# Deferring the layernorm scale of two tiles, loading on two queues and sending two biases later in a fused attention/MLP kernel

## The chip, the cores and the metric

The kernel runs on one core of one Trainium2 chip. The metric is the device time of one execution in microseconds (us), taken as the median of several runs. A core has five instruction streams that run side by side and wait for each other through semaphores: TensorE (PE, matmuls; PEld is its weight load), VectorE (DVE), ScalarE (ACT), GpSimd (POOL) and SyncE (SP). SP does no arithmetic here; it issues DMA transfers. ACT can issue DMA transfers too, between its activations. An issuing stream waits in order: what stands behind a waiting DMA on the same stream waits with it.

## What is computed

The input x has 2048 rows of 512 numbers, all in float32. It is normalised row by row, and two branches use the result:

```python
xn = _layernorm(x)                                # (x - mean) / sqrt(var + 1e-5)
q, k, v = split(xn @ wqkv)                        # 32 heads of 16
logits = q . k[pos - 2*w] * 16**-0.5              # w = 0..7, a dilated window
s = (softmax(logits) . v[pos - 2*w]) @ wo
h = relu(xn @ w1 + b1) ** 2                       # 512 -> 1792
g = silu(h @ w2 + b2)
return x + s * g
```

A row's layernorm is a subtraction of its mean and a multiplication by one number, rs = (var + 1e-5)^-0.5. A matmul is linear, so the multiplication may be done before the matmul or on its result.

## The kernel before

The rows of x are handled as 16 tiles of 128 rows, called t = 0 to 15, and in pairs; "pair 10" is tiles 10 and 11 (`pair` and `pair_of_seven` are called with a = 2, 4, ... 14; tiles 0 and 1 stand ahead of them, written out by hand). Stage one makes q, k and v of every tile, pair by pair. Stage two is the MLP with the output projection, in four chunks of four tiles. The attention itself (products, softmax and sums on DVE, a generator called `attention`) is woven between the PE work of both stages: `pump` lets as much of it be issued as a running estimate of PE's and DVE's time allows.

Matmul operands are split into a high and a low part (fp32r), and each product is three passes over these parts; `high` is an ACT copy that rounds, `low` a subtraction on DVE or POOL, `split` both.

How a tile of stage one is made: `load_x` brings 128 rows; `bn_stats` and `bn_aggr` on DVE give mean and variance (`mv`); DVE adds 1e-5, POOL raises to -0.5 (`rs`); DVE subtracts the mean and multiplies by rs (`xn`). For tiles 0 to 3, PE then transposes xn into PSUM (`pxT`, a matmul with the identity `ident`), and ACT and DVE write the high and low part of the transposed tile into `xT[0]` (tiles 0 to 3 in one buffer, used again at the start of stage two by `up(0, f)`). For tile 0 the transposed tile is first copied out as plain float32, `x0` (xT0f in the profile), and the first product of the program, k of tile 0, is made of it and of the raw weights `wqraw1_0` to `wqraw1_3` (four pieces of the k columns, 128 rows of wqkv each): 8 matmuls of the group pq<-wqraw,xT0f. The transposes of tile 1 stand ahead of the last piece. `evacuate` copies a product from PSUM to a staging tile `stg` on ACT, and `store_qkv` sends pairs of tiles to the DRAM scratch tensors `sq`, `sk`, `sv`, from which `load_u` loads the attention's operands on ACT's queue. PE starts with `WARM` transposes of the identity into an unused bank while it waits for the first tile.

Every operation of PE, DVE, ACT and POOL passes through `Ordered`, which keeps it in program order on its engine; a helper records them, so they all have line 91 in the profile. Transfers sent with `queue` keep program order on SP as well. Those sent with `dma` alone may be moved ahead by the scheduler: b1 and b2 are written in the program after pair 12 (a == NT - 4), and in the profile SP issues them at about 10 us. `plan` is a table of what is done beside which step of which pair: `at(a, step, f, ...)` puts a call behind the PE work of that step. `next_w` (pairs 12 and 14, then in stage two) splits one block of w1 and w2, the low parts on POOL, and asks for a later block.

Of the kernel before, what the change touches and what calls it, by code (L numbers as in the profile page):

```python
# [15 lines left out]
P = 128  # L16
S = 2048
D = 512
# [28 lines left out]
WARM = 18  # L47
# [12 lines left out]
def body(ctx: ExitStack, tc: tile.TileContext, x, wqkv, wo, w1, b1, w2, b2, out):  # L60
# [103 lines left out]
    def load_wq(s, kt, tag=None):  # L164
        rows = wqkv[kt * P:(kt + (2 if tag else 1)) * P, s * 512:(s + 1) * 512]
        if tag is None:
            raws[s, kt] = piece(f"wqraw{s}_{kt}")
            dma(raws[s, kt], rows)
            return
        if kt == 0:  # L170
            raws[s] = att.tile([P, KT, 512], F32, name=f"wqraw{s}", tag=tag)
        dma(raws[s][:, kt:kt + 2], rows.rearrange("(k p) n -> p k n", p=P))
        for i in (kt, kt + 1):
            raws[s, i] = raws[s][:, i]
# [7 lines left out]
    load_wq(1, 0)  # L182
    load_x(1)
    for kt in range(1, KT):
        load_wq(1, kt)
# [19 lines left out]

    b1t = const.tile([P, NF], F32, name="b1t")
    b2t = const.tile([P, D], F32, name="b2t")

    sq = dram.tile([GR, S, CH], F32, name="sq")
# [236 lines left out]

    def norm(t):
# [9 lines left out]
        if t < STATS:  # L457
            halves = [slice(0, D // 2), slice(D // 2, D)] if t == 0 else [slice(None)]
            for i in halves:
                V.tensor_scalar(dst[:, i], src[:, i], mv[t][:, 0:1], rs[t], op0=OP.subtract, op1=OP.mult)  # L460
        else:
            A.activation(dst, src, AF.Identity, bias=shifts.pop(t), scale=rs[t])
        if t < 2:
            load_x(t + 4)
# [115 lines left out]
    def evacuate(t, s, ps, new=True):  # L580
        if t % 2 == 0 and new:
            new_stg(t, s)
        A.activation(stgs[s][:, :, t % 2], ps.rearrange("p (g c) -> p g c", g=GR), AF.Copy)
        if t % 2:
            store_qkv(t, s)
# [52 lines left out]
    stats(0)  # L638
    high(*wq_parts(1, 0))
    norm(0)  # L640
# [5 lines left out]
    stats(1)  # L646
# [6 lines left out]
    norm(1)  # L653
# [113 lines left out]
    at(8, 1, lambda u: start("v", u), 0)  # L767
    plan.setdefault((10, 2), []).append((release, "k"))
# [111 lines left out]
    for a in range(2, NT, 2):  # L880
        if a >= TPC:
            for t in (a, a + 1):
                queue(sx[t // TPC][:, :, t % TPC], xts[t].bitcast(F32))
        (pair_of_seven if a in SEVEN else pair)(a)
        if a == NT - 4:
            dma(b1t, b1.rearrange("(f p) -> p f", p=P))
            dma(b2t, b2[None, :].to_broadcast([P, D]))
# [203 lines left out]
```

## Time and profile before

| | us |
|---|---|
| median of 3 runs | 485.36 (485.15 to 486.0) |
| the profiled execution | 485.13 |
| its span (first to last instruction) | 483.1 |

| engine | busy us | share of the span |
|---|---|---|
| DVE | 423.0 | 88% |
| ACT | 240.0 | 50% |
| POOL | 225.3 | 47% |

The profile is of one execution; 2.0 us of its time lie outside the span. Times in the rows below are counted from the span's start. In a row of the timeline, the first number is the start, the second the time taken (of several instructions together when an x2 or more stands behind), then the engine, the line, the operation and output<-input; in brackets stands how long the engine was idle before and what it then waited for. SPq and ACTq are the issues of DMA transfers by SP and ACT; their time is that of the issue, not of the transfer. PE records overlap, since a matmul's end is modelled: the start of the next one tells more than the sum.

### The profile page before, as it was taken

How to read it: one execution, taken by the hardware profiler on the slowest of the kernel's cores; microseconds unless marked ns; L12 is line 12 of the kernel's file. 1: busy time of each engine (PE TensorE's matmuls, PEld its weight loads, DVE VectorE, ACT ScalarE, POOL GpSimd, SP SyncE). 2: the span in 40 equal slices, each digit the busy share in tenths (PEclk: the TensorE clock that was granted, in tenths of full speed). 3: DMA queues.
4: the chain of work that ended last, by engine and by line, in shares of the span. 5: the costliest groups of instructions: out<-in, count | busy, mean ns of one | idle time of the engine just before them, and what ended most of it. 6: DMA issues, size and time to landing. Idle time of an engine off the chain costs nothing.

```text
span 483.1 us, 6128 instructions
## 1 busy us (share of the span) xinstructions
PE 477.4 (99%) x2190; PEld 396.6 (82%) x2190; DVE 423.0 (88%) x352; ACT 240.0 (50%) x441; POOL 225.3 (47%) x178
## 2 busy tenths in 40 slices
PE   8999999999999999999999999999999999999996
PEld 5888888888888888888888888888888888888885
DVE  5978999899499899999999999999999999889133
ACT  5548798856566565273513345342234543423240
POOL 1459853116986699436543322434433345253210
PEclk9999999999999999999999999999999999999999
DMA  7899999998779996571627548071707725220321
GB/s 283 243 251 258 277 243 302 263 306 269 209 198 228 255 224 151 178 166 43 170 72 185 115 164 190 26 189 43 197 16 196 224 48 145 43 86 27 87 105 71
DMA packets 71002, 81.47 MB, mean 169 GB/s; under 512 B 6204, under 2 KB 55612, under 8 KB 70972
## 3 DMA queue, kind: packets, MB, share of 16 engines
q1 hardware_dynamic: 65788, 54.87, 41.3%
q10 hardware_dynamic: 5184, 26.22, 21.8%
q8 instruction: 17, 0.28, 0.2%
q14 instruction: 13, 0.11, 0.1%
HBM read 50.60 MB, written 27.32 MB: 161 GB/s over the span
## 4 chain that ended last, share of the span: by engine, by line
PE 98%; DMA 1%; DVE 0%; POOL 0%; issue 0%; ACT 0%; POOLq 0%
PE ph L91 32%; PE pb L91 32%; PE pm L91 12%; PE pq L91 9%; PE pw L91 9%; PE pv L91 4%; DMA x<-in_A_x 1%; PE pxT L91 0%; DVE z L91 0%; DVE st L91 0%; POOL rs L91 0%; DVE xn L91 0%; ACT xT0f L91 0%; DVE mv L91 0%; DVE rs L91 0%
## 5 line engine op out<-in xcount | busy, mean ns | idle before, releaser
L91 PE MATMUL pb<-w,h 128*128 128x512 f32 x672 | 160.1, 389 | 0.0
L91 PEld LDWEIGHTS pb<-w,h 128*128 128x128 f32 x672 | 126.1, 188 | 26.2
L91 POOL TENSOR_TENSOR h<-hf,h 128x512 fp32r<-128x512 f32 x46 | 67.7, 1473 | 157.5 <-ACT hf L91 157.5
L91 PE MATMUL ph<-xU,w 128*128 128x512 f32 x504 | 120.2, 389 | 0.0
L91 ACT ACTIVATE ph<-ph,b1t 128x512 f32<-128x512 f32 x56 | 37.0, 661 | 153.9 <-PE ph L91 144.0
L91 PEld LDWEIGHTS ph<-xU,w 128*128 128x128 f32 x504 | 94.6, 188 | 19.6
L91 DVE TENSOR_TENSOR pr<-k,q 128x2048 f32<-128x2048 f32 x32 | 78.7, 2460 | 3.2 <-DMA q<-sq 2.5
L91 DVE TENSOR_TENSOR pv<-v,L 128x2048 f32<-128x2048 f32 x32 | 77.3, 2417 | 3.8 <-POOL L L91 3.1
L91 DVE TENSOR_REDUCE L<-pr 128x128 f32<-128x2048 f32 x32 | 73.0, 2281 | 0.7
L91 DVE TENSOR_REDUCE v<-pv 128x256 f32<-128x2048 f32 x32 | 72.9, 2279 | 0.7
L91 PE MATMUL pw<-wot,oT 128*128 128x512 f32 (+1 forms) x204 | 45.9, 376 | 0.0
L91 PEld LDWEIGHTS pw<-wot,oT 128*128 128x128 f32 x204 | 36.8, 188 | 7.1
L91 POOL TENSOR_TENSOR w<-w1r,w 128x512 fp32r<-128x512 f32 x14 | 31.6, 2259 | 23.4 <-ACT w L91 23.2
L91 PE MATMUL ph<-xT,w 128*128 128x512 f32 x168 | 40.0, 389 | 0.0
L91 PEld LDWEIGHTS ph<-xT,w 128*128 128x128 f32 x168 | 31.5, 188 | 6.6
L91 PE MATMUL pm<-wq,S 128*128 128x512 f32 x144 | 36.8, 392 | 0.0
L91 ACT ACTIVATE h<-ph 128x512 fp32r<-128x512 f32 x56 | 33.5, 599 | 1.8
L91 PE MATMUL pq<-wq,xT 128*128 128x512 f32 x132 | 30.9, 393 | 0.0
L91 PEld LDWEIGHTS pm<-wq,S 128*128 128x128 f32 x144 | 26.2, 188 | 5.3 <-DVE S L91 0.4
L91 PEld LDWEIGHTS pq<-wq,xT 128*128 128x128 f32 x132 | 24.5, 188 | 5.9 <-ACT xT L91 0.7
L91 ACT ACTIVATE hf<-ph 128x512 f32<-128x512 f32 x46 | 27.4, 595 | 1.9 <-POOL h L91 1.9
L91 PE MATMUL pm<-wq,xt 128*128 128x512 f32 x108 | 27.6, 392 | 0.0
(96 smaller groups left out, 531.0 us busy)
## 6 DMA issues: line engine op xcount, KB each, us to landing
k<-sk ACTq DMA_DIRECT2D x8, 960.0 KB, 7.1
v<-sv ACTq DMA_DIRECT2D x8, 960.0 KB, 7.4
sx<-xt SPq DMA_DIRECT2D x12, 512.0 KB, 5.8
xU<-sx ACTq DMA_DIRECT2D x12, 512.0 KB, 5.9
x<-in_A_x SPq DMA_DIRECT2D x16, 256.0 KB, 6.4
sk<-stg SPq DMA_DIRECT2D x8, 512.0 KB, 4.3
sq<-stg SPq DMA_DIRECT2D x8, 512.0 KB, 7.5
sv<-stg SPq DMA_DIRECT2D x8, 512.0 KB, 5.0
```

The source lines that it names most:

```text
L91: return tc.keep_in_program_order(f(*a, **k))
```

## The change

1. Tiles 0 and 1 are made by `centre` in place of `stats` and `norm`: the mean is subtracted and nothing is multiplied. `deviation` makes rs after that, in a column of a new tile `scales`, and sends the column to a DRAM scratch row `rows_dram` (128 elements of 4 bytes).
2. `evacuate` multiplies q, k and v of these two tiles by rs on the way out of PSUM (a scale operand of the ACT copy).
3. `up(0, f)` still needs the normalised tiles, transposed, where rs lies along the free axis. So SP loads both rows of rs back, broadcast to all partitions (`rows`). At pair 10 `rescale` adds high and low part of a tile's transposed x on POOL (`full`) and multiplies by the row, also on POOL; at pair 12 `rescaled` splits the result into `xT[0]` again, high on ACT and low on POOL.
4. The four raw pieces of the k columns go on two queues: 0 and 2 on ACT's, ahead of its table load, 1 and 3 on SP's, behind x of tiles 0 and 1.
5. WARM goes from 18 to 15.
6. b1 and b2 are sent with `queue`, at the end of pair 10 (a == NT - 6).

```diff
@@ -44,7 +44,7 @@
 SEVEN = range(4, 16, 2)
 VSEVEN = range(6, 14, 2)
 
-WARM = 18
+WARM = 15
 WARM2 = 3
 
 TURN = 4
@@ -161,11 +161,11 @@
 
     raws = {}
 
-    def load_wq(s, kt, tag=None):
+    def load_wq(s, kt, tag=None, send=dma):
         rows = wqkv[kt * P:(kt + (2 if tag else 1)) * P, s * 512:(s + 1) * 512]
         if tag is None:
             raws[s, kt] = piece(f"wqraw{s}_{kt}")
-            dma(raws[s, kt], rows)
+            send(raws[s, kt], rows)
             return
         if kt == 0:
             raws[s] = att.tile([P, KT, 512], F32, name=f"wqraw{s}", tag=tag)
@@ -179,10 +179,9 @@
 
 
     load_x(0)
-    load_wq(1, 0)
     load_x(1)
-    for kt in range(1, KT):
-        load_wq(1, kt)
+    for kt in range(KT):
+        load_wq(1, kt, send=queue if kt % 2 else A.dma_start)
     for kt in (0, 2):
         load_wq(0, kt, "pr")
     load_x(2)
@@ -203,9 +202,12 @@
         for w in range(W - 1):
             G.memset(mask[:GR, :(W - 1 - w) * DIL, w], -1e9)
 
+    scales = const.tile([P, 2], F32, name="scales")
+    rows = const.tile([P, 2 * P], F32, name="rows")
     b1t = const.tile([P, NF], F32, name="b1t")
     b2t = const.tile([P, D], F32, name="b2t")
 
+    rows_dram = dram.tile([2, P], F32, name="rows_dram")
     sq = dram.tile([GR, S, CH], F32, name="sq")
     sk = dram.tile([GR, HALO + S, CH], F32, name="sk")
     sv = dram.tile([GR, HALO + S, CH], F32, name="sv")
@@ -444,6 +446,38 @@
         V.bn_stats(st, xins[t])
         moments(t, st)
 
+    def centre(t):
+
+        st = px.tile([P, 6], F32, name=f"st{t}", tag="st", bufs=2)
+        mv[t] = px.tile([P, 2], F32, name=f"mv{t}", tag="mv", bufs=2)
+        xn[t] = dst = px.tile([P, 2, D], F32, name=f"xn{t}", tag="xb", bufs=2)[:, 0]
+        src = xins.pop(t)
+        V.bn_stats(st, src)
+        V.bn_aggr(mv[t], st)
+        halves = [slice(0, D // 2), slice(D // 2, D)] if t == 0 else [slice(None)]
+        for i in halves:
+            V.tensor_scalar(dst[:, i], src[:, i], mv[t][:, 0:1], None, op0=OP.subtract)
+        load_x(t + 4)
+
+    def deviation(t):
+        rs[t] = scales[:, t:t + 1]
+        V.tensor_scalar_add(rs[t], mv[t][:, 1:2], 1e-5)
+        G.tensor_tensor(rs[t], rs[t], mhalf, op=OP.pow)
+        dma(rows_dram[t:t + 1, :].rearrange("a p -> p a"), rs[t])
+
+    fulls = {}
+
+    def rescale(t):
+
+        if t == 0:
+            dma(rows, rows_dram.rearrange("a p -> (a p)")[None, :].to_broadcast([P, 2 * P]))
+        fulls[t] = full = px.tile([P, KT, P], F32, name=f"full{t}", tag="x", bufs=4)
+        G.tensor_add(full, xt[t][:, 0].bitcast(F32), xt[t][:, 1].bitcast(F32))
+        G.tensor_mul(full, full, rows[:, None, t * P:(t + 1) * P].to_broadcast([P, KT, P]))
+
+    def rescaled(t):
+        split(xt[t][:, 0], xt[t][:, 1], fulls[t], G)
+
     def norm(t):
 
         src = xins.pop(t)
@@ -455,13 +489,9 @@
             dst = xn[t // 2 * 2][:, :, t % 2].rearrange("p a (k c) -> p k a c", k=KT)
             src = src.rearrange("p (k a c) -> p k a c", a=4, k=KT)
         if t < STATS:
-            halves = [slice(0, D // 2), slice(D // 2, D)] if t == 0 else [slice(None)]
-            for i in halves:
-                V.tensor_scalar(dst[:, i], src[:, i], mv[t][:, 0:1], rs[t], op0=OP.subtract, op1=OP.mult)
+            V.tensor_scalar(dst, src, mv[t][:, 0:1], rs[t], op0=OP.subtract, op1=OP.mult)
         else:
             A.activation(dst, src, AF.Identity, bias=shifts.pop(t), scale=rs[t])
-        if t < 2:
-            load_x(t + 4)
 
     def place(t):
         if t < TPC:
@@ -580,7 +610,8 @@
     def evacuate(t, s, ps, new=True):
         if t % 2 == 0 and new:
             new_stg(t, s)
-        A.activation(stgs[s][:, :, t % 2], ps.rearrange("p (g c) -> p g c", g=GR), AF.Copy)
+        scale = dict(scale=rs[t]) if t < 2 else {}
+        A.activation(stgs[s][:, :, t % 2], ps.rearrange("p (g c) -> p g c", g=GR), AF.Copy, **scale)
         if t % 2:
             store_qkv(t, s)
 
@@ -635,22 +666,22 @@
         low(*wq_parts(s, kt + 1), V)
 
 
-    stats(0)
+    centre(0)
     high(*wq_parts(1, 0))
-    norm(0)
+    deviation(0)
     xT[0] = xTa.tile([P, KT, TPC, 2, P], FR, name="xT0", tag="xT")
     place(0)
     pT = [psT(f"pxT0_{kt}") for kt in (0, 2)]
     for kt in range(KT):
         PE.transpose(pT[kt // 2][:, kt * P:(kt + 1) * P], xn[0][:, kt * P:(kt + 1) * P], ident)
-    stats(1)
+    centre(1)
+    deviation(1)
     low(*wq_parts(1, 0), V)
 
     x0 = hpool.tile([P, D], F32, name="xT0f", tag="h", bufs=4)
     for kt in (0, 2):
         cols = slice(kt * P, (kt + 2) * P)
         A.activation(x0[:, cols], pT[kt // 2][:, cols], AF.Copy)
-    norm(1)
     for kt in range(1, KT):
         split(*wq_parts(1, kt), V)
     high(xt[0][:, 0], None, x0.rearrange("p (k n) -> p k n", k=KT))
@@ -765,6 +796,9 @@
     for i in range(2):
         at(4, i, load_w, i)
     at(8, 1, lambda u: start("v", u), 0)
+    for t in range(2):
+        at(10, 1 + 3 * t, rescale, t)
+        at(12, 3 + t, rescaled, t)
     plan.setdefault((10, 2), []).append((release, "k"))
     plan.setdefault((10, 4), []).append((release, "q"))
 
@@ -882,9 +916,9 @@
             for t in (a, a + 1):
                 queue(sx[t // TPC][:, :, t % TPC], xts[t].bitcast(F32))
         (pair_of_seven if a in SEVEN else pair)(a)
-        if a == NT - 4:
-            dma(b1t, b1.rearrange("(f p) -> p f", p=P))
-            dma(b2t, b2[None, :].to_broadcast([P, D]))
+        if a == NT - 6:
+            queue(b1t, b1.rearrange("(f p) -> p f", p=P))
+            queue(b2t, b2[None, :].to_broadcast([P, D]))
     pump()
     lowh(1)
     p1ctx.close()
```

The change moves instructions at three places. The first is DVE's first rows, from the first tile's statistics on (st, mv: statistics of a tile; rs or scales: the factor; wq: high and low parts of weights). Before:

```order
L91 BN_STATS st0_155<-x0_121 128x6
L91 BN_AGGR mv0_157<-st0_155 128x2
L91 TENSOR_SCALAR rs0_158<-mv0_157 128x1
L91 TENSOR_SCALAR xn0_163<-x0_121,mv0_157,rs0_158 128x256 x2
L91 BN_STATS st1_175<-x1_125 128x6
L91 BN_AGGR mv1_177<-st1_175 128x2
L91 TENSOR_SCALAR rs1_178<-mv1_177 128x1
L91 TENSOR_TENSOR wq2_113<-wqraw1_0_123,wq2_113 128x512
L91 TENSOR_SCALAR xn1_186<-x1_125,mv1_177,rs1_178 128x512
```

And now:

```order
L91 BN_STATS st0_155<-x0_118 128x6
L91 BN_AGGR mv0_156<-st0_155 128x2
L91 TENSOR_SCALAR xn0_157<-x0_118,mv0_156 128x256 x2
L91 TENSOR_SCALAR scales_143<-mv0_156 128x1
L91 BN_STATS st1_175<-x1_120 128x6
L91 BN_AGGR mv1_176<-st1_175 128x2
L91 TENSOR_SCALAR xn1_177<-x1_120,mv1_176 128x512
L91 TENSOR_SCALAR scales_143<-mv1_176 128x1
L91 TENSOR_TENSOR wq2_110<-wqraw1_0_122,wq2_110 128x512
```

The centred tile now follows its mean at once, and the factor is made behind it, for tile 1 ahead of the first split of weights.

The second is SP's queue from x of tile 4 to the first store of k (sk). Before:

```order
L104 DMA x4_166<-in_A_x 128x512
L104 DMA x5_188<-in_A_x 128x512
L886 DMA b1t_146<-in_B_b1 128x14x1
L887 DMA b2t_147<-in_B_b2 128x512
L104 DMA sk_149<-stg0_1_210 128x8x128
```

And now:

```order
L104 DMA x4_162<-in_A_x 128x512
L466 DMA rows_dram_147<-scales_143 128x1
L104 DMA x5_181<-in_A_x 128x512
L466 DMA rows_dram_147<-scales_143 128x1
L473 DMA rows_144<-rows_dram_147 128x256
L104 DMA sk_149<-stg0_1_210 128x8x128
```

The two bias loads are gone from here (they stand 48 rows further on, behind the last store of pair 10), and the two stores of rs and the load that reads them back have taken their place ahead of the store of k.

The third is POOL from the last statistics of pair 10 to the weights of pair 14 (w0, w1: blocks of w1 and w2; stg: sums for k and v). Before:

```order
L91 TENSOR_TENSOR shift15_1028<-mean15_1026,rs15_1027 128x1
L91 TENSOR_TENSOR stg10_1_1086<-stg10_1_1086,stg10_0_1088 128x8x64
L91 TENSOR_TENSOR stg10_2_1087<-stg10_2_1087 128x4x64
L91 TENSOR_TENSOR w0_1320<-w1r0_593,w0_1320 128x512
L91 TENSOR_TENSOR w0_1320<-w2r0_594,w0_1320 128x512
L91 TENSOR_TENSOR stg12_1_1234<-stg12_1_1234,stg12_0_1236 128x8x64
L91 TENSOR_TENSOR stg12_2_1235<-stg12_2_1235 128x4x64
L91 TENSOR_TENSOR w1_1411<-w1r1_631,w1_1411 128x512
```

And now:

```order
L91 TENSOR_TENSOR full0_1150<-xT0_168 128x512
L91 TENSOR_TENSOR full0_1150<-full0_1150,rows_144 128x512
L91 TENSOR_TENSOR stg10_1_1086<-stg10_1_1086,stg10_0_1088 128x8x64
L91 TENSOR_TENSOR stg10_2_1087<-stg10_2_1087 128x4x64
L91 TENSOR_TENSOR full1_1217<-xT0_168 128x512
L91 TENSOR_TENSOR full1_1217<-full1_1217,rows_144 128x512
L91 TENSOR_TENSOR w0_1329<-w1r0_593,w0_1329 128x512
L91 TENSOR_TENSOR w0_1329<-w2r0_594,w0_1329 128x512
L91 TENSOR_TENSOR stg12_1_1243<-stg12_1_1243,stg12_0_1245 128x8x64
L91 TENSOR_TENSOR stg12_2_1244<-stg12_2_1244 128x4x64
L91 TENSOR_TENSOR xT0_168<-full0_1150,xT0_168 128x4x128
L91 TENSOR_TENSOR xT0_168<-full1_1217,xT0_168 128x4x128
```

Six operations are added: two ahead of pair 10's sums, two behind them, and two between pair 12's sums and the weights of pair 14.

## The prediction

> **What bounds the kernel now.** I read the page first, then the busy times by stage, then the chain of waits.
>
> ```profile
> PE 477.4 (99%) x2190; PEld 396.6 (82%) x2190; DVE 423.0 (88%) x352; ACT 240.0 (50%) x441; POOL 225.3 (47%) x178
> PE 98%; DMA 1%; DVE 0%; POOL 0%; issue 0%; ACT 0%; POOLq 0%
> 12.00:24.00 12.00, 12.00 (x58) 9.75 (x57) 11.28 (x26) 7.04 (x14) 4.85 (x13) 1.00 0.89 244
> 450.00:483.10 33.10, 29.26 (x141) 24.54 (x139) 8.67 (x14) 9.38 (x15) 3.87 (x3) 1.00 0.24 83
> ```
>
> In the stage rows the first pair after the stretch is PE's busy time. PE sets the end: it is full from 12 us on and loses 3.8 us in the last stretch, which the change doesn't touch. No matmul of use is removed. So the change can gain only what it takes from the head, and lose only where it makes PE wait later. The head, from the chain of waits:
>
> ```profile
> 0.73 2.71 DMA x<-in_A_x
> 3.47 0.70 DVE st L91
> 4.19 0.19 DVE mv L91
> 4.41 0.17 DVE rs L91
> 4.72 0.57 POOL rs L91
> 5.31 0.42 DVE xn L91
> 5.78 0.46 PE pxT L91 x2
> 6.26 0.39 ACT xT0f L91
> 6.70 2.84 PE pq L91 x6
> 9.54 0.48 PE pxT L91 x4
> 10.02 6.55 PE pq L91 x26
> ```
>
> x of tile 0 lands, its statistics go through DVE and POOL, the tile is normalised, transposed, copied, and PE starts its first product at 6.70. From there PE works on end: everything behind moves with that start.
>
> **The head, step by step.** The factor rs leaves the chain: xn can start where rs started, at 4.41 in place of 5.31. That is **-0.90**.
>
> Against it stand three prices. The rows for them:
>
> ```profile
> 1.35 4.10 PE L91 MATMUL warm<-ident 128*128 128x128 f32 x18 [1.35 <-POOL mhalf L91]
> 4.29 0.63 ACT L91 ACTIVATE wq<-wqraw 128x512 fp32r<-128x512 f32 x1 [2.28 <-DMA wqraw<-in_A_wqkv]
> 6.53 0.69 DVE L91 BATCH_NORM_STATS2 st<-x 128x6 f32<-128x512 f32 x1 [0.48 <-DMA x<-in_A_x]
> 7.21 1.98 ACT L91 ACTIVATE wq<-wqraw 128x512 fp32r<-128x512 f32 x3 [0.25 <-DMA wqraw<-in_A_wqkv]
> 7.23 0.19 PEld L91 LDWEIGHTS pq<-wqraw,xT0f 128*128 128x128 f32 x1 [0.24 <-DMA wqraw<-in_A_wqkv]
> 9.39 0.63 PE L91 MATMUL pxT<-ident,xn 128*128 128x128 f32 x4
> 15.14 0.99 PEld L91 LDWEIGHTS pq<-wq,xT 128*128 128x128 f32 x5 [0.23 <-DVE wq L91]
> 3.50:7.00 3.50, 3.02 (x15) 2.25 (x14) 2.20 (x6) 1.33 (x3) 0.56 (x1) 1.00 0.79 259
> 7.00:14.50 7.50, 7.50 (x29) 4.57 (x28) 6.92 (x16) 6.40 (x12) 0.96 (x1) 1.00 1.04 391
> ```
>
> First, x of tile 0 now shares the DMA engines from its first byte with the first weight piece, which ACT issues at the same time; before, that piece was issued behind it. Lower end: x lands as now, 0. Upper end: x lands where that piece did, 4.29 against 3.47, or 0.82. An issue took 0.59 on ACT and 0.38 on SP in the rows on SP's queue below, so x keeps a lead of some 0.2; I take **+0.25**, nearer the lower end.
>
> Second, the second weight piece. The first product would then start at 6.70 - 0.90 + 0.25 = 6.05, and its second piece is wanted 0.53 later (6.70 to 7.23 now), at 6.58. In the kernel before PE and ACT waited for that piece until 7.2, as the fourth transfer of SP's queue. It is now the third, and the third landed at 6.53 (x of tile 1, for which DVE waited 0.48). That covers it: **0**. Upper end: it is the fifth of both queues together; a 256 KB transfer takes 0.67 us at 391 GB/s and 1.0 at 259, so it would land at 7.9 to 8.2, PE would start the second piece 0.7 to 1.0 later than before, and the whole gain would be gone. For the lower end speaks that the engines were busy 0.79 of the time and moved 259 GB/s from 3.5 to 7.0 us with loads waiting behind, but 391 after: with one queue they were not full.
>
> Here a rule of the Trainium skill speaks against the change: DMA: Bandwidth & Descriptors, section "Issuing engines are not separate DMA queues", has all issuing engines feed the same 16 DMA engines, so a second queue saves only the time to issue. By that rule the piece comes fifth and the sum is a loss of about 0.85; the row's 259 against 391 GB/s leaves it open, and it stands as a rival below.
>
> Third, PE's speed. The 18 warm transposes took some 0.22 each (4.10 us), the four at 9.39 some 0.12 to 0.16 each: PE was at half speed at first and doubled in between. Four transposes moved 0.65 earlier may still be slow: 0 to 0.2 on the path; I take **+0.1**. Three warm ones fewer free PE at about 4.8 (1.35 + 15 x 0.22 and the last one's drain), ahead of the centred tile (4.41 + 0.42 + 0.25 = 5.1), so they delay nothing; that PE speeds up later because of it is a rival.
>
> From 6.70 on the chain is PE's rows without a gap (6.70, 9.54, 10.02): tile 1's shorter chain gains nothing of its own. It gives DVE time back, and PE's 0.23 wait for DVE at 15.14 may go; I count 0, and 0.2 in the best case.
>
> **SP's queue.** The bias loads leave the head and three small transfers come, the last of which waits for the round trip of the second store. SP's next work is the first store of k.
>
> ```profile
> 11.27 4.25 SPq L887 DMA_DIRECT2D b2t<-in_B_b  x1
> 15.62 0.38 SPq L104 DMA_DIRECT2D sk<-stg  x1
> 20.39 0.59 ACTq L91 DMA_DIRECT2D k<-sk  x1
> 23.01 0.60 ACT L91 ACTIVATE stg<-pq 128x512 f32<-128x512 f32 x1 [2.12 <-PE pq L91]
> b2t<-in_B_b SPq DMA_DIRECT2D x1, 256.0 KB, 7.3
> sk<-stg SPq DMA_DIRECT2D x1, 512.0 KB, 4.5
> ```
>
> Before, b2's issue held SP to 15.52. If the second store of rs goes out as late as that issue began, 11.27, and lands 7.3 later as b2 did, the read goes at 18.6, k's store at 19.0, and it lands 4.5 later at 23.5 instead of 20.1. ACT, which waits there to issue the load of k, has 2.12 idle behind it, so its next copy is about 1 us late; PE has three more accumulator banks and doesn't notice. **0**; with that cover gone, 1 us. At pair 10 the biases hold SP for 5 us or so (b2's 4.25 again), and the next load it has to issue there, w1, waits for POOL until 114.05: 0.
>
> **Pairs 10 to 14.** POOL gets six more operations of 128x512, ACT two copies and six scaled evacuations.
>
> ```profile
> 97.08 1.29 POOL L91 TENSOR_TENSOR stg<-stg,stg 128x512 f32<-128x512 f32 x1 [9.38 <-ACT stg L91]
> 111.01 3.04 POOL L91 TENSOR_TENSOR w<-w1r,w 128x512 fp32r<-128x512 f32 x1 [11.92 <-ACT w L91]
> 116.97 1.19 POOL L91 TENSOR_TENSOR stg<-stg 128x256 f32<-128x256 f32 x1
> 119.79 2.29 DVE L91 TENSOR_TENSOR pr<-k,q 128x2048 f32<-128x2048 f32 x1
> 120.17 3.07 POOL L91 TENSOR_TENSOR w<-w1r,w 128x512 fp32r<-128x512 f32 x1 [2.01 <-ACT w L91]
> 132.93 0.60 ACT L91 ACTIVATE hf<-ph 128x512 f32<-128x512 f32 x1 [1.54 <-POOL h L91]
> 133.42 0.59 ACT L91 ACTIVATE stg<-pm 128x512 f32<-128x512 f32 x1
> 134.87 1.52 PE L91 MATMUL pm<-wq,xt 128*128 128x512 f32 x6
> 100.33 1.28 DVE L91 TENSOR_TENSOR S<-Sf,S 128x512 fp32r<-128x512 f32 x2
> 102.51 1.52 PE L91 MATMUL pm<-wq,S 128*128 128x512 f32 x6
> ```
>
> A POOL operation of this size takes 1.29, and 3.07 where a DVE multiplication of two tiles in SBUF runs: they exclude each other, and either may wait. The first two pairs of operations fall into POOL's idle 9.38 and 11.92. The second of these, at 99.1 to 101.7, meets DVE's S at 100.33, whose first half PE wants at 102.51 + 2 x 0.23 = 2.0 after it ended (1.28 / 2 behind 100.33): one POOL operation of 1.29 ahead of it is covered, two cost 0.6.
>
> The last two come between 118.16 and 120.17, in an idle 2.01, and want 2 x 1.29 = 2.58. The second one then runs into DVE's pr at 119.79, which starts at 120.74 and ends at 123.0; POOL's next weights end at 123.0 + 1.29 = 124.3, not 123.24: POOL is 1.05 late, with weights queued up behind. ACT waits for POOL's h at the end of that queue (1.54 at 132.93), then evacuates pm at 133.42 to 134.01, and PE wants that bank at 134.87: 0.86 of cover. So 0 to 0.2; I take **+0.1**.
>
> **The sum:** -0.90 + 0.25 + 0.1 + 0.1 = -0.45. The profiled execution took 485.13 (a span of 483.1 and 2.0 around it), which gives 484.68; the median of the runs, 485.36, lies 0.23 above it, so **484.9** for the median. Differences under 0.2%, or 0.97 us, can hardly be told from no change here.
>
> **The rivals.** (1) *The whole head is won*: x of tile 0 lands as before, the second queue fills the engines, POOL's delay stays covered, and the wait at 15.14 goes: -0.90 - 0.2, 484.3. For it: the half-empty engines until 7.0. Against it: two transfers start together. (2) *The second queue adds nothing*: the second piece lands fifth, +0.85 with no gain left, 486.2. For it: the transfers share one set of engines, as the traffic of one stage has one rate. (3) *POOL's last two operations*, slower: if all 2.58 or, with both behind DVE multiplications, 2 x 3.07 = 6.1 less the idle 2.0 = 4.1 go to the chain, PE waits 1.7 to 3.3 at its product at 134.87. Less the head's 0.55 that is 486.5 to 488.1. It decides from a delay of 2.4 on (0.86 of cover, 0.55 of gain, 0.97 to be seen). Against it: the two fall beside reductions for the most part. (4) *PE stays slow*: the warm stretch is now 15 x 0.22 = 3.3 us with a gap of 0.3 to 0.8 behind it. If the doubling comes one such stretch later, at about 10 us, PE does the 4 us from 6 to 10 at half speed, +2.0, 486.9. Against it: before, too, there was a gap of 0.3 ahead of the first transposes.
>
> TensorE: Matmul & The Clock Gate in the Trainium skill, part 1, states that PE runs at half clock until about 3.4 us of sustained activity, in a window that runs freely; 15 transposes are at that edge, and 18 were above it. The trace agrees that the rate doubles some 4 us after the first matmul; by the rule, a late doubling can strike some executions and not others.
>
> **The chances.** The forecast 0.47, its own range 484.4 to 485.6; rival 1 0.25; rival 2 0.10; rival 3 0.10; rival 4 0.08. Faster by over 0.2%: rival 1 and the forecast's edge, 0.27. Slower: rivals 3 and 4, 0.18. Within: 0.55. The range for 8 in 10 cuts off the edges of rival 1 and the upper ends of 3 and 4: 484.0 to 486.7.
>
> **What would show it.** Right: xn right behind mv, no POOL row in the chain; first product at about 6.15, k of tile 1 at 10.2; in pair 14 the same gapless PE. Wrong: statistics of tile 0 at 4.2 or later (first price), a PE load waiting for wqraw after the first two matmuls (rival 2), pxT rows and first matmuls at twice their time (rival 4), an idle PE between 102 and 139 (rival 3), or ACT's load of k so late that q's load, and with it the first products of attention, move back.

## The result and the profile after

| | before | after |
|---|---|---|
| median of 5 runs each, us | 485.67 (485.15 to 486.0) | 491.06 (490.31 to 491.92) |
| ratio, with 95% interval | | 1.011 (1.0096 to 1.0125) |
| the profiled execution, us | 485.13 | 491.06 |
| its span, us | 483.1 | 489.2 |

The change made the kernel 5.4 us slower; 484.9 was predicted. The span grew by 6.1 us. To see where, each matmul's start in the profile after is set against the start of the same matmul before. The difference, PE's delay below, grows in three places: to 1.95 by 10.7 us, to 4.6 between 42 and 48 us (pair 4; 0.3 of it is made good at 59 us), and from 4.4 to 6.2 between 158 and 192 us (second stage). Then it stays.

The rows of busy time by stage carry the same. Columns: the stretch, its length, busy time of PE, PEld, DVE, ACT and POOL, PEclk, the DMA engines' share and their GB/s. The kernel before:

```profile
0.00:12.00 12.00, 10.17 (x40) 6.93 (x41) 6.72 (x15) 6.70 (x12) 2.25 (x9) 1.00 0.79 282
...
36.00:48.00 12.00, 12.00 (x55) 9.93 (x54) 9.84 (x15) 9.79 (x22) 10.83 (x13) 1.00 0.96 254
...
150.00:200.00 50.00, 50.00 (x222) 41.39 (x222) 47.16 (x32) 29.35 (x52) 37.46 (x22) 1.00 0.83 197
```

The kernel after:

```profile
0.00:12.00 12.00, 9.61 (x30) 6.24 (x31) 5.29 (x13) 4.75 (x8) 2.23 (x9) 1.00 0.85 319
12.00:24.00 12.00, 12.00 (x55) 9.17 (x55) 10.86 (x23) 8.48 (x15) 4.07 (x12) 1.00 0.38 95
...
36.00:48.00 12.00, 10.41 (x45) 7.68 (x43) 8.17 (x17) 6.52 (x14) 9.32 (x9) 1.00 0.89 278
...
150.00:200.00 50.00, 49.68 (x215) 39.48 (x214) 44.09 (x31) 27.66 (x51) 41.35 (x24) 1.00 0.85 208
...
450.00:489.20 39.20, 35.44 (x168) 29.67 (x166) 13.07 (x19) 12.82 (x21) 5.16 (x4) 0.99 0.25 81
```

At the end PE is idle for 3.76 us, much as before (3.84). From 12 to 24 us the DMA engines moved 95 GB/s; before they moved 244. And PE, full from 36 to 48 us before, now lacks 1.6 us there. The lost time in the head is for the most part not an idle PE but a slow one. PEclk doesn't show it, since it is the mean over what the trace's clock record covers, and that begins at 10.48 here (5.64 before). The timeline of PE, after, shows the speed itself:

```profile
1.35 3.46 PE L91 MATMUL warm<-ident 128*128 128x128 f32 x15 [1.35 <-POOL mhalf L91]
5.81 1.12 PE L91 MATMUL pxT<-ident,xn 128*128 128x128 f32 x4 [0.99 <-DVE xn L91]
6.97 4.57 PE L91 MATMUL pq<-wqraw,xT0f 128*128 128x512 f32 x6
```

The four transposes took 1.12 instead of 0.76, and six matmuls 4.57 instead of 2.84: PE was at half speed until about 10.5, where before it doubled at 5.64. DVE's row of tile 0's statistics shows the late x, "st<-x" now at 4.45 instead of 3.47, and xn right behind mv:

```profile
4.45 0.69 DVE L91 BATCH_NORM_STATS2 st<-x 128x6 f32<-128x512 f32 x1 [4.45 <-DMA x<-in_A_x]
...
5.40 0.61 DVE L91 TENSOR_SCALAR xn<-x,mv 128x256 f32<-128x256 f32 x2
```

So rs left the chain as meant (0.9 gained), x landed 0.98 later, and the first product began at 6.97 instead of 6.70.

**Pair 4.** SP's issues in the timeline after:

```profile
9.73 0.33 SPq L466 DMA_DIRECT2D rows_dram<-scales  x1
20.40 0.33 SPq L473 DMA_DIRECT2D rows<-rows_dram  x1
20.82 0.39 SPq L104 DMA_DIRECT2D sk<-stg  x1
...
29.83 7.64 SPq L104 DMA_DIRECT2D x<-in_A_x  x4
```

The DMA view from 0 to 40 us, in 40 slices of 1 us (GB/s), and the time from issue to landing of the transfers that read `scales`, the two stores of rs (shortest, median, longest):

```profile
GB/s 0 14 248 322 404 402 410 406 408 406 406 410 406 388 95 0 0 0 0 0 0 7 54 193 325 339 281 244 93 146 309 184 239 157 157 219 360 273 323 410
```

```profile
DMA to landing us min/median/max: 10.6/11.6/12.5
```

And the timeline of the engines that wait, ACT, DVE and PE, with one piece of the chain of waits, the first load of x from its issue to its landing:

```profile
27.17 0.60 ACTq L91 DMA_DIRECT2D k<-sk  x1
27.82 1.27 ACT L91 ACTIVATE stg<-pq,scales 128x512 f32<-128x512 f32 x2 [4.81 <-PE pq L91]
...
29.83 10.64 DMA x<-in_A_x
...
40.49 0.69 DVE L91 BATCH_NORM_STATS2 st<-x 128x6 f32<-128x512 f32 x1 [2.40 <-DMA x<-in_A_x]
...
45.65 1.19 PE L91 MATMUL pm<-wq,xt 128*128 128x512 f32 x4 [1.18 <-DVE xt L91]
```

The second store of rs, 512 bytes as 128 elements of 4 bytes, was issued at 9.73 and took 10.6 us to land; in the trace its last packet ran at 14.6, so 5.7 of these passed behind it. SP stood until 20.40 to issue the read of the row, and everything behind it in SP's queue stood too: from 15 to 21 us no transfer ran at all. The store of k went at 20.82 instead of 15.62, the load of k at 27.17 instead of 20.39. Four loads of x stand behind. In the kernel before, the timeline of SP and DVE has them so:

```profile
28.58 1.90 SPq L104 DMA_DIRECT2D x<-in_A_x  x4
...
33.56 0.70 DVE L91 BATCH_NORM_STATS2 st<-x 128x6 f32<-128x512 f32 x1 [0.38 <-DMA x<-in_A_x]
...
36.68 0.69 DVE L91 BATCH_NORM_STATS2 st<-x 128x6 f32<-128x512 f32 x1 [2.02 <-DMA x<-in_A_x]
```

There the first two were issued at 28.58 and 28.98, and DVE had them at 33.56 and 36.68. Now the first was issued at 29.83, only 1.25 later, but it took 10.64 us to land instead of 4.96, and DVE had it at 40.49. What moved beside it is the load of k: before, that one had landed at 28.18, ahead of the first x; now it was under way from 27.17 to 36.17. It also held up the other three: by the trace's semaphores SP issued the second at 36.18, when the load of k had landed, since it waits on the semaphore that this load sets. DVE had the second x at 41.51. Behind the two stood the transposed tiles of pair 4 (the first at 44.92 instead of 40.03), for which PE then waited.

The other profiles bear this out. In the six with both stores and the read in the head, the first x took 9.8 to 11.1 us with the load of k still moving; with only the stores there (a_read_late below) it took 9.3; in the eight others the load of k had landed 0.4 to 0.8 before that x was issued, and it took 4.1 to 5.5.

**Second stage.** Pieces of the chain of waits after, in order of time, and the waits from 155 to 194 us:

```profile
147.50 3.36 POOL w L91
150.87 8.54 DMA w2r<-in_B_w
...
159.43 0.52 ACTq L91
...
162.67 3.01 PE ph L91 x12
```

```profile
DVE h L91 <- ACT ph L91: 4.3, 1, 4.3
...
PEld ph L91 <- DVE h L91: 2.5, 6, 0.5
```

POOL's split of weights ends late, SP issues the next w2r behind it at 150.87, and that transfer takes 8.54. ACT's next instruction is the issue of the load of q, which waits until it has landed (159.43), and DVE stands 4.3 for ACT. What this delay then costs is seen in DVE's timeline:

```profile
173.03 0.68 DVE L91 TENSOR_TENSOR h<-ph,h 128x512 fp32r<-128x512 f32 x1
173.63 2.27 DVE L91 TENSOR_REDUCE L<-pr 128x128 f32<-128x2048 f32 x1
175.94 2.98 DVE L91 TENSOR_TENSOR pr<-k,q 128x2048 f32<-128x2048 f32 x1
178.84 0.68 DVE L91 TENSOR_TENSOR h<-ph,h 128x512 fp32r<-128x512 f32 x1
```

One round of DVE takes 5.81 (173.03 to 178.84), one of PE 5.44 (two groups of 12 matmuls, 2.72 each). Before, DVE came into this stretch with enough lead; now it comes late, and each round takes 0.2 to 0.4 from PE: 1.77 between 155 and 195 us.

### The profile page after: what moved, and what is told of

Read it like the earlier page. It is cut to its first block, busy times and chain, and to the rows that moved or that the text cites. A ratio compares the mean times of both kernels' runs of the same rounds, so it can differ in the third digit from the quotient of the medians.

```text
span 489.2 us, 6136 instructions
## 1 busy us (share of the span) xinstructions
PE 481.1 (98%) x2187; PEld 396.3 (81%) x2187; DVE 423.8 (87%) x352; ACT 241.1 (49%) x443; POOL 247.3 (51%) x184
## 4 chain that ended last, share of the span: by engine, by line
PE 78%; DMA 7%; DVE 5%; POOL 5%; issue 3%; ACT 1%; SPq 0%; ACTq 0%; DVEq 0%; POOLq 0%
PE pb L91 27%; PE ph L91 26%; PE pm L91 10%; PE pw L91 9%; PE pv L91 4%; DMA x<-in_A_x 3%; POOL w L91 3%; DMA w2r<-in_B_w 2%; PE pq L91 2%; DMA sq<-stg 1%; DVE L L91 1%; DVE h L91 1%; DVE st L91 1%; DMA w1r<-in_B_w 1%; POOL xT L91 1%
## 5 line engine op out<-in xcount | busy, mean ns | idle before, releaser
L91 POOL TENSOR_TENSOR h<-hf,h 128x512 fp32r<-128x512 f32 x46 | 76.7, 1667 | 145.4 <-ACT hf L91 142.2
```

The costliest lines, as they stand in the source:

```text
L91: return tc.keep_in_program_order(f(*a, **k))
```

## The experiments

The theory: three independent losses, (1) PE's doubling comes late because fewer warm transposes and the late x leave a gap, (2) SP's wait for the round trip of rs, (3) POOL's rescaling, or the biases, in the second stage. The rivals are named with each run. The kernel before ran beside them, with medians of 485.27 to 485.91 over 13 to 22 runs. "Delay" is PE's delay against the profile before, just ahead of pair 4 (41 us), behind it (70 us), at 155 us and at 195 us; "doubling" is the time from which PE stays at full speed in the head, by the trace's clock record.

| kernel | median (runs), us | ratio (95%) | doubling | delay at 41 | 70 | 155 | 195 |
|---|---|---|---|---|---|---|---|
| after | 491.06 (5) | 1.011 (1.0096 to 1.0125) | 10.48 | 2.00 | 4.31 | 4.41 | 6.18 |
| b_warm15 | 486.87 (10) | 1.0016 (0.9999 to 1.0033) | 10.60 | 1.90 | 1.68 | 1.68 | 1.91 |
| a_warm18 | 490.4 (4) | 1.0096 (1.0076 to 1.0117) | 4.16 | -0.15 | 3.09 | 3.16 | 4.53 |
| a_rows_late | 491.67 (4) | 1.0112 (1.0082 to 1.0141) | 5.23 | -0.11 | -0.39 | 6.74 | 6.74 |
| a_read_late | 488.67 (4) | 1.0056 (1.0035 to 1.0077) | 9.67 | 1.43 | 2.17 | 3.63 | 4.29 |
| a_bias_early | 491.1 (4) | 1.0102 (1.0064 to 1.0139) | 4.41 | 0.12 | 3.85 | 3.98 | 6.25 |
| a_no_pool | 488.88 (8) | 1.0057 (1.0037 to 1.0076) | 4.37 | 0.12 | 4.10 | 4.10 | 4.10 |
| a_one_queue | 490.46 (5) | 1.0096 (1.0065 to 1.0128) | 6.47 | -0.52 | 3.51 | 3.61 | 4.63 |
| b_two_queues | 487.92 (10) | 1.0036 (1.0009 to 1.0062) | 11.72 | 2.45 | 2.53 | 2.53 | 4.40 |
| a_no_trip | 486.33 (10) | 0.9998 (0.9981 to 1.0015) | 9.65 | 1.48 | 1.47 | 1.47 | 1.47 |
| f1 | 486.26 (12) | 1.0009 (0.9995 to 1.0024) | 6.52 | -0.09 | 0.70 | 0.69 | 1.11 |
| b_warm20 | 486.67 (12) | 1.0015 (0.9997 to 1.0033) | 5.16 | -0.10 | -0.10 | -0.10 | 1.50 |
| a_q_first | 488.6 (4) | 1.006 (1.0041 to 1.0079) | 10.47 | 1.95 | 3.49 | 3.58 | 5.24 |
| b_q_first | 485.91 (12) | 1.0012 (0.9999 to 1.0026) | 5.75 | -0.05 | -0.14 | -0.14 | -0.07 |

In b_two_queues PE was fast from 4.90 to 8.31 and slow again until 11.72. Where the runs fall into two groups, the ratio can differ by up to 0.16% from the quotient of the medians; its interval is what counts.

### The warm-up (b_warm15, a_warm18)

```diff
-WARM = 18
+WARM = 15
```

on the kernel before, and the reverse on the changed one.

> The kernel before with WARM 15 in place of 18 and nothing else. Theory (clock): in the changed kernel's profile PE ran at half speed to 10.5 us because 15 warm transposes leave too long a gap ahead of tile 0's. Here the gap is as long (4.6 to 5.8), so PE's first products should again stand 0.85 apart and not 0.43, and the time should rise by 1.0 to 2.0 us, to 486.7 to 487.7. Rival (chance): when PE doubles its rate is set by a phase that has nothing to do with the number of warm transposes; then 485.7, as before.

> The changed kernel with WARM 18 again. Theory (clock): the first products run at full speed, k of tile 1 starts some 1.7 us earlier than 12.67, and the time falls from 491.1 to about 489.4. Rival (the late first tile): the gap that x's late landing leaves is what counts, and three more transposes don't close it: 491.1.

The profile of the kernel before with 15 transposes shows PE's slow head alone, +1.9, with x landing as before:

```profile
6.93 4.64 PE L91 MATMUL pq<-wqraw,xT0f 128*128 128x512 f32 x6
```

Over its ten runs it is a matter of chance: three at 484.9 to 485.5, the rest from 486.0 to 487.9, and the interval of the ratio reaches below 1, so the runs alone don't show a rise. With 18 the changed kernel had its doubling at 4.16 and no delay in the head, and still took 490.4: the delay behind pair 4 was 3.1. (The profiled run, 489.41, is the fastest of its four.) So the head's loss and pair 4's don't simply add. A PE that comes 2 us earlier waits longer there for the transfers.

### The round trip (a_rows_late, a_read_late)

The stores and the read of rs moved to pair 8, each sent by a small function in SP's order (a_rows_late), or the read alone (a_read_late, without the lines on the stores):

```diff
-        dma(rows_dram[t:t + 1, :].rearrange("a p -> p a"), rs[t])
...
-        if t == 0:
-            dma(rows, rows_dram.rearrange("a p -> (a p)")[None, :].to_broadcast([P, 2 * P]))
...
+    at(8, 4, send_rows, 0)
+    at(8, 4, send_rows, 1)
+    at(8, 5, read_rows, 0)
```

> The changed kernel with both stores of rs and the load that reads them back moved to pair 8 in SP's queue. Theory (round trip): they hold up the first store of k, with it ACT, the loads of x and of q, and make PE wait 2.4 us at pair 4; here that wait is gone, the store of k is issued near 17 and not 20.8, and the time is 488.7, unless the round trip now holds SP in pair 8. Rival (scaled evacuations and the lost 2 us of the head make pair 4 late): the wait at pair 4 stays, 490.5 to 491.

> The changed kernel with the two stores of rs where they are, and only the load that reads them back moved to pair 8. It parts two forms of the round-trip theory. If SP's wait for the stores is what costs, the store of k is issued near 17 and the time is 488.7, as with both moved. If the stores themselves clog the DMA engines (in the profile x of tile 5 and both stores land only at 20 with hardly any traffic from 14 to 20), the store of k is issued early but lands no earlier than 24, and the time stays at 490 to 491.

With both late, the wait at pair 4 is gone (delay -0.11 to -0.39), and the loss is at 98 to 112 us instead (one of the four runs took 488.98, the others 491.6 to 492.0). Its waits there:

```profile
POOL full L91 <- DMA rows<-rows_dram: 14.1, 1, 14.1
ACT stg L91 <- POOL stg L91: 6.6, 1, 6.6
...
PE pv L91 <- ACT stg L91: 3.4, 2, 3.1
```

POOL stood 14.1 us for the row, ACT behind POOL, PE behind ACT; and after that gap PE ran at half speed from 107.6 to 114.4, PEclk 0.50 in the busy time by stage:

```profile
100.00:107.60 7.60, 5.46 (x30) 4.55 (x28) 7.57 (x8) 1.02 (x3) 4.72 (x3) 1.00 0.95 251
107.60:114.40 6.80, 5.80 (x20) 5.13 (x21) 2.58 (x5) 3.69 (x9) 3.27 (x3) 0.50 1.14 331
```

With only the read late, SP doesn't stand (the store of k goes at 15.91), and pair 4 costs 0.74 instead of 2.3: two thirds of it was SP's wait. The 0.74 that stays goes with the stores of 4-byte elements: the load of k was issued at 22.39 and landed at 32.58, again beside the first x. The median agrees with the 488.7 expected, but in part by chance: PE lost another 1.46 between 70 and 155 us, 1.1 of it at 118 to 121, after POOL had stood 7.9 us for the row at 91 to 99. The way from there to PE isn't shown.

### The second stage (a_bias_early, a_no_pool)

```diff
-        if a == NT - 6:
-            queue(b1t, b1.rearrange("(f p) -> p f", p=P))
-            queue(b2t, b2[None, :].to_broadcast([P, D]))
+        if a == NT - 4:
+            dma(b1t, b1.rearrange("(f p) -> p f", p=P))
+            dma(b2t, b2[None, :].to_broadcast([P, D]))
```

in a_bias_early, and in a_no_pool:

```diff
     def rescale(t):
...
+        return
...
     def rescaled(t):
-        split(xt[t][:, 0], xt[t][:, 1], fulls[t], G)
+        pass
```

> The changed kernel with b1 and b2 sent at pair 12, by the queue that takes turns, as before; all else as changed. The changed kernel showed a third loss of 1.75 us between 158 and 191 us, in steps of 0.25 to 0.37 at which the products ph wait for DVE's h. Theory A (the biases, sent two pairs earlier in SP's queue, hold back the load of w2r, which landed 8.54 us after its issue): the steps go, the offset of PE against the kernel before is the same at 195 us as at 155, and the time falls by 1.5 to 2 us. Rival B (POOL's rescaling of tiles 0 and 1 makes POOL late for the splits of the weights): the steps stay, and the time is within 0.5 us of the changed kernel's 491.06.

> The changed kernel without POOL's sums, products and splits of the two tiles' transposed x (the row of rs is stored and read back as changed; the transposed x of tiles 0 and 1 stays centred but unscaled for the second stage, which this kernel so leaves out). Theory B (POOL): the steps of 158 to 191 us go, and the time falls by 1.5 to 2 us to 489.0 to 489.6. Rival A (the biases at pair 10): the steps stay, and the time is within 0.5 us of 491.06. The wait at pair 4 stays in both cases, since the round trip through memory is kept.

The biases' place is not it: 491.1, and the second stage lost 2.3. Without POOL's work it lost nothing, and the median fell by 2.2. (a_no_pool leaves out ACT's two copies for the splits as well; that POOL is the one is read from the waits.) The way there begins in SP's issues behind the store of v. The timeline after:

```profile
141.73 0.53 SPq L104 DMA_DIRECT2D sv<-stg  x1
144.57 0.37 SPq L406 DMA_DIRECT2D w1r<-in_B_w  x1
```

And without POOL's work:

```profile
140.71 0.53 SPq L104 DMA_DIRECT2D sv<-stg  x1
141.69 0.47 SPq L406 DMA_DIRECT2D w1r<-in_B_w  x1
```

The next weights are asked for 2.84 behind the store of v instead of 0.98: SP waits there for POOL to free their buffer. Of the seven profiled kernels with POOL's rescaling six lost 0.7 to 2.3 us between 155 and 195 us (a_rows_late didn't).

The trace's semaphores show what this lateness meets. In all thirteen profiles in which, at 145 to 152 us, the load of k is issued ahead of that of q, ACT issued the load of q 0.02 to 0.03 us after one load of w2r had landed, on whose semaphore it waits. They fall into three groups (times in us):

| profiles | that w2r was issued | and took | q issued behind k by | lost between 155 and 195 |
|---|---|---|---|---|
| before, b_warm15, a_rows_late, a_no_pool, a_no_trip, f1 | 1.16 to 1.22 before k | 3.29 to 3.62 | 2.15 to 2.42 | 0 to 0.42 |
| b_warm20, b_two_queues | 1.22 before k | 5.43, 6.10 | 4.23, 4.91 | 1.60, 1.87 |
| a_read_late, a_one_queue, a_warm18, after, a_bias_early | 1.09 to 1.16 behind k | 7.29, 7.77, 8.52, 8.54, 9.04 | 8.42 to 10.15 | 0.66, 1.02, 1.37, 1.77, 2.27 |

With POOL late, this w2r comes behind the load of k (960 KB) instead of ahead of it and takes 4 to 6 us longer, and ACT stands at the issue of q for that time. In the last group the loss rises with it. a_rows_late has the rescaling, but its w2r came ahead of k, and it lost nothing there.

Pair 4 in a_no_pool, whose head lost nothing, by the timeline of PE and then the busy time:

```profile
44.83 1.66 PE L91 MATMUL pm<-wq,xt 128*128 128x512 f32 x4 [2.25 <-DVE xt L91]
```

```profile
45.30:48.70 3.40, 3.40 (x10) 2.15 (x9) 2.36 (x5) 3.07 (x8) 3.23 (x5) 0.50 0.89 178
```

PE came on time, waited 2.25, and soon after ran at half speed for 3.4 us. So an early PE lost as much at pair 4 as the late one lost in head and pair 4 together.

### The two queues (a_one_queue, b_two_queues)

```diff
+    load_wq(1, 0, send=queue)
     load_x(1)
-    for kt in range(KT):
-        load_wq(1, kt, send=queue if kt % 2 else A.dma_start)
+    for kt in range(1, KT):
+        load_wq(1, kt, send=queue)
```

in a_one_queue; b_two_queues does the reverse to the kernel before.

> The changed kernel with the first loads in the order of the kernel before and on SP's queue alone. Theory C (x of tile 0 shares the engines with the first piece that ACT sends at the same time): x of tile 0 lands at 3.4 to 3.6 instead of 4.42, and the first product starts 0.7 to 1.0 earlier, at 6.0 to 6.3; the time falls by 0.7 to 1.0 if the clock doubles as late as in the changed kernel, by up to 2.5 if it doubles early. Rival (x of tile 0 lands late for another reason, such as its place in the queue): the landing stays above 4.2. The wait at pair 4 stays.

> The kernel before with only the first loads changed to two queues. Theory C (shared engines): x of tile 0 lands 0.8 to 1.1 later, at 4.2 to 4.5, and since x leads the chain to the first product here too, the first product starts 0.8 to 1.1 later, at 7.5 to 7.8 instead of 6.70; the time is 486.1 to 486.7 with an early doubling of the clock. Rival (the loads in sum come sooner, and the chain from x is not the longest): the first product is within 0.2 of 6.70 and the time within 0.3 of 485.5.

The changed kernel with one queue, DVE and PE:

```profile
3.40 0.69 DVE L91 BATCH_NORM_STATS2 st<-x 128x6 f32<-128x512 f32 x1 [3.40 <-DMA x<-in_A_x]
...
5.92 3.10 PE L91 MATMUL pq<-wqraw,xT0f 128*128 128x512 f32 x6
```

The kernel before with two queues:

```profile
4.37 0.69 DVE L91 BATCH_NORM_STATS2 st<-x 128x6 f32<-128x512 f32 x1 [4.37 <-DMA x<-in_A_x]
...
6.68 0.77 PE L91 MATMUL pxT<-ident,xn 128*128 128x128 f32 x4 [1.44 <-DVE xn L91]
```

x of tile 0 lands 0.9 to 1.05 later with two queues, in either kernel: it is the second queue that makes it late. Over all profiles DVE had it at 4.13 to 4.52 with two queues (nine) and at 3.38 to 3.56 with one (six). With one queue the change does bring its product forward, to 5.92, and PE is 0.52 ahead at 41 us. Pair 4 takes it: the delay behind is 3.5, and the median falls by 0.6, less than the 0.7 to 2.5 expected. In b_two_queues the first product came at 7.59, as expected; its 487.92 lies above the 486.1 to 486.7 given for an early doubling, which its profile doesn't have. It also lost 1.87 in the second stage, with no rescaling in it; DVE there waited 4.6 for q, against 2.5 before. Of the eight profiled kernels without the rescaling this and b_warm20 (below) lost over 0.5 us there. So POOL is not the only way into this loss.

### Without the trip, and a version from the findings (a_no_trip, f1)

a_no_trip takes away both stores, the read and the rescaling. f1 is the kernel before with these lines:

```diff
-WARM = 18
+WARM = 15
-    stats(0)
+    centre()
...
-    norm(0)
...
+    PE.transpose(pT[1][:, 0:P], rs[0].to_broadcast([P, P]), ident)
+    A.activation(rows, pT[1][:, 0:P], AF.Copy)
+    G.tensor_mul(x0s.rearrange("p (k n) -> p k n", k=KT), x0.rearrange("p (k n) -> p k n", k=KT),
+                 rows[:, None, :].to_broadcast([P, KT, P]))
```

`centre` treats tile 0 alone, its k is scaled where it leaves PSUM, and x0s is split in place of x0.

> The changed kernel without the two stores of rs, the read of the row and POOL's rescaling: tiles 0 and 1 stay unscaled in the second stage, which this kernel so leaves out. What is left of the change is the head, the scaled evacuations and the place of the biases. If the losses at pair 4 and in the second stage come from the round trip and from POOL's rescaling alone, PE's offset against the kernel before stays below 0.3 us from 12 us to the end, apart from what the clock does in the head: a span of 482.9 to 483.6 where the clock doubles by 6.5 us, 484.7 to 485.4 where it doubles after 9.5. If the scaled evacuations or the biases have a share in the losses, a step of 0.5 us or more is left at 42 to 48 us or at 158 to 191 us.

> A version built from the findings: the kernel before with first loads on one queue as before, tile 0 alone centred first, its k scaled where it leaves PSUM, 15 warm-up transposes (so that PE goes from them to tile 0's without a gap); the row of rs is made by one transpose of rs in the head, and POOL scales the transposed x of tile 0 there, before it is split, so that there is no trip through memory and no later rescaling. Expected: first transposes at 4.8 instead of 5.78, first product at 6.0; k of tile 1 at 10.0 to 10.4 instead of 10.71 where the clock doubles by 6.5 us; no wait at pair 4 or in the second stage; 484.8 to 485.2, that is 0.3 to 0.6 below the kernel before. The rival is that the trip over POOL makes the split of tile 0 late for its q at 12.7 us, and PE gives the gain back there: 485.4 to 486.5.

Without the trip and the rescaling nothing is left of the losses but the head's doubling: the delay is 1.48 at 41 us and 1.47 at 195. Four of its ten runs lie at 484.86 to 485.28, where the faster runs of the kernel before lie too. So losses 2 and 3 of the changed kernel belong to trip and rescaling, and what is left of the change, with its late x, gains nothing that can be told (0.9981 to 1.0015).

f1 had its first product at 5.90 and was no faster. Its lead, 0.80 there, was 0.44 at the last matmul of tile 0's k (PE doubled at 6.52 instead of 5.64, and the transpose of rs stood between), and gone at the next (10.73 against 10.71), for which PE waited 0.30 for ACT, whose copy stood behind POOL's product. It then fell 0.8 behind at 44 and 59 us, where PE waited for S:

```profile
10.73 5.51 PE L91 MATMUL pq<-wq,xT 128*128 128x512 f32 x23 [0.30 <-ACT xT L91]
...
59.50 1.19 PE L91 MATMUL pm<-wq,S 128*128 128x512 f32 x4 [0.25 <-DVE S L91]
```

### What else spreads the runs (b_warm20, a_q_first, b_q_first)

b_warm20 is the kernel before with

```diff
-WARM = 18
+WARM = 20
```

and the other two are the changed kernel and the kernel before with

```diff
-                yield from load(u + 1, "kq")
+                yield from load(u + 1, "qk" if u == 1 else "kq")
```

> The kernel before with 20 warm-up transposes, which at 0.213 us each fill PE to 5.87 us, past tile 0's xn at 5.78: no gap is left. If the clock doubles at the end of a stretch of some 3.41 us, at a phase that differs by execution, in which PE was nearly without a gap (doublings seen: 4.2 to 6.5, or 9.7 to 10.6 where a gap of 0.7 to 1.0 lay in the stretch before), it now doubles by 7.7 us at the latest: the slower group of runs at 486.25 to 487.5, about a quarter of the runs of the kernel before, goes, and all runs lie within 484.8 and 486.2, the median at 485.0 to 485.6. If the spread has another cause, the slower group stays at its share of a quarter.

> The changed kernel with one pair of issues on ACT swapped: the load of q of the third unit (in the profiles at 148 to 160 us) ahead of the load of k, which stood just before it. In the kernels whose second stage lost time, the load of q was issued 4.2 to 10.2 us after that of k, against 2.2 to 2.4 in the others; theory D: the load of k starts while the store of q is still in SP's queue and takes the engines from it, the load of q waits for that store, ACT and DVE stand, and DVE's rounds of 5.8 us then hold PE, whose rounds take 5.44. With q first the store meets no load of k: q is issued within 1 us of where PE's own delay puts it (by 153), the steps between 158 and 191 us go, PE's offset at 195 us is within 0.3 of that at 150, and the time is 489.0 to 489.6. Rival E (the store of q is late because POOL's rescaling holds SP's queue, whatever the load of k does): q is issued 3 us late or more, now with k behind it, and the steps stay or grow: 490.8 to 493.

> The kernel before with the same swap. Theory D: it loses nothing where the store of q landed in time anyway, and the runs in which the second stage lost 1.5 us (as in the profiled runs with two queues and with 20 warm-up transposes) go: the median falls by 0 to 0.4, and the share of runs above 486.2 from a third to the share of late doublings of the clock, a fifth or less. Rival: the load of k, now 2.4 us later, lands after DVE wants it, and the time rises by 0.5 to 2 us.

b_warm20 missed: no gap was left worth the name (0.21) and the doubling came at 5.16, but its slower runs stayed. Its profile has the second stage's loss, 1.6, with DVE's wait as in b_two_queues:

```profile
DVE pr L91 <- DMA q<-sq: 4.7, 1, 4.7
PEld ph L91 <- DVE h L91: 2.2, 5, 0.5
```

So two things can differ by execution without the change, the doubling and this; the profile of the kernel before itself shows neither. a_q_first was to show that the load of k delays the store of q. q was issued at 148.87, in time, as the theory had it, yet the delay grew by 1.66 between 155 and 195 us, since ACT now waited 8.3 for w2r and DVE 4.3 for ACT: the theory that the order of these two loads makes the loss falls. The same w2r was issued behind both loads, at 149.98, and took 10.4. The median of a_q_first, 2.5 below the changed kernel's, rests on four runs in two groups (487.5 to 487.6, 489.6 to 490.4) and isn't explained. b_q_first changed nothing that can be told. By the table above, the transfer that decides whether DVE comes late to the second stage is that load of w2r; what stays open is why it took 5.4 and 6.1 us in the two profiles without rescaling, ahead of the load of k as in those that took 3.3 to 3.6. No version that beats the kernel before was found.

## Why the prediction was wrong

- **The head's gain, -0.90:** right. xn stands right behind mv, and no POOL row is in the chain.
- **The first price, +0.25 for x of tile 0:** too small; it measured 0.98, above the upper end of 0.82. The working gave x a lead of 0.2 from the times of issue. With two queues DVE had x 0.66 to 1.05 later than the 3.47 of before in each profile, with one queue on time, so most or all of the gain went here.
- **The second piece, 0:** right. PE waited for no wqraw, and the engines moved 319 GB/s in the first 12 us instead of 282. Rival 2 falls. The rule set beside it (the Trainium skill, DMA: Bandwidth & Descriptors, "Issuing engines are not separate DMA queues") was taken to mean that the piece comes fifth and late, which these rows don't show.
- **PE's speed, +0.1:** wrong in this execution; rival 4, with a chance of 0.08, came true, and its +2.0 was +1.7. Its condition was half seen: the doubling comes at a different time in each execution, and a gap behind the warm transposes goes with the late one: of nine profiles with a gap of 0.67 to 1.22 five doubled at 9.65 or later (not the two longest), of five with 0.41 or less none did. The late x widened the gap to 0.99, and the working never joined these two terms. The Trainium skill, TensorE: Matmul & The Clock Gate, part 1, has the freely running window of about 3.4 us; the half-speed stretch of 3.4 us in a_no_pool and the doublings between 4.2 and 11.7 agree with it.
- **SP's queue, "0; with that cover gone, 1 us":** the step that failed. It had the round trip nearly right, the read at 18.6 (20.40 measured) and the store of k at 19.0 (20.82). It then followed one transfer, the store and load of k, to ACT's idle time, and found cover. It stopped at the issue of the load of k (27.17 instead of 20.39) and didn't follow it to its landing, nor the queue behind: that load was now under way until 36.17, beside the first load of x, which landed at 40.47 instead of 33.54, and ahead of the other three, which SP could issue only when it had landed. PE has no cover for those. In this execution that was 2.3 us, and 3.2 to 4.0 where PE came on time.
- **Pairs 10 to 14, +0.1:** right for where it looked; PE lost 0.1 from 70 to 155 us. Rival 3 had POOL's work coming out at 134.87, in the products of stage one. It came out 25 us later, through a chain that wasn't in the working: POOL late, its buffers late, SP's load of w2r behind the load of k instead of ahead of it, ACT held at the issue of q until it landed, DVE late, and DVE's rounds of 5.81 against PE's 5.44. It measured 1.77.
- **The sum** put three losses beside each other that are not independent: head and pair 4 together were 3.1 to 4.3 in every kernel with the early trip, whatever the head did.

## What to carry to other kernels

A small transfer that a queue waits for costs what stands behind it in that queue, so a round trip through memory is priced by listing every later issue of its queue, each to its landing and its consumer, and not the next one alone. Transfers that come late also move beside others and make them slow, and an issue may wait on the semaphore of a transfer whose data it doesn't need, as x waited here for k, and q for w2r. When a kernel's engines keep each other busy, a lead won at the start is kept only if the transfers come earlier too; otherwise PE waits out the difference at the next load. Work put on an engine with idle time may come out far behind, where what it frees is asked for again.

## What the runs showed of the hardware

- A store of 128 elements of 4 bytes each, one from each partition, took 10.6 us to land, the one ahead of it 12.5; the last packet of the two ran at 14.6 (after), and in the last 5 us no transfer ran. In a_rows_late, at 86 us, the two took 10.5 and 10.3.
- At pair 4, pauses of PE of 1.79 (a_bias_early), 2.25 (a_no_pool) and 2.35 us (a_one_queue) went with half speed for 3.4 us, from 0.3 before PE's return to 1.0 behind it; one of 3.14 (a_rows_late, at 105 us) went with 6.8 us. Pauses of 1.18 (after) and 1.54 (a_warm18) at pair 4 brought none, while one of 1.44 in the head of b_two_queues was followed by 3.4 us at half speed, from 1.6 behind PE's return. Length alone doesn't decide it. A wait in the middle of the program can thus cost more than its length.
- With 15 or 18 warm transposes PE came to full speed for good anywhere from 4.16 (a_warm18) to 11.72 us (b_two_queues). With that, one profile tells nothing of a change in the head of 2 us.
